# Attention and MLP on one core: two early transfers placed later, and split transfers halved by partitions

## The chip, the core and the metric

The kernel runs on one core of a Trainium2 chip. TensorE (PE) multiplies matrices, ScalarE (ACT) and VectorE (DVE) work on tiles in the on-chip memory of 128 partitions, and SyncE (SP) issues the transfers, which 16 DMA engines carry out. The metric is the device time of one execution in microseconds (us); the median of three is compared.

## The reference

Attention with a sigmoid in place of the softmax, on 8 batches and 12 heads of 448 x 64, then an MLP with a sigmoid-weighted middle. The weights and tensors arrive as follows: q, k and v as float32, the two weight matrices as float64.

```python
scores = scale * np.matmul(q, k.transpose(0, 1, 3, 2)) - np.log(S)
attn = 1.0 / (1.0 + np.exp(-scores))
attn_out = np.matmul(attn, v)                      # (8, 12, 448, 64)
x = attn_out.transpose(0, 2, 1, 3).reshape(3584, 768)
h = x @ w_in                                       # 768 x 2048
g = h * (1.0 / (1.0 + np.exp(-1.702 * h)))
out = g @ w_out                                    # 2048 x 768
```

## The kernel before, in words

Heads are taken in pairs: `pairs` counts (b, p), batch and pair within the batch, six pairs to a batch. Two pairs are a unit. A pair's query and key rows arrive as one tile `qkraw` of 128 partitions and 896 columns (`load_pair`), which ACT or DVE rounds and DVE completes with the rest (`split_pair`, tile `qk`). The pair numbers in names: `qkraw_5` is the sixth pair of batch 0, the `qkraw_0` behind it the first of batch 1, so the seventh pair. The values of a unit's four heads are one tile `vraw`, so `vraw_4` is the third unit's.

PE computes scores (`sc`) in groups of six matmul instructions into four PSUM banks in turn; ACT turns each bank into a tile of sigmoids (`a`, `aside`) at line 709; PE multiplies these by the values (`av`, lines 800 and 780). A unit's scores stand in a long run of seven groups, 42 instructions, and the value matmuls behind it. A group can begin when the bank that it writes has been read by its sigmoid, so the fifth group needs the first sigmoid of the run, the sixth the second, the seventh the third, and the first value matmuls (line 800) the fourth.

Beside attention the weights are decoded from float64 (`decode`): a tile `w_8`, `w_9`, ... of 128 partitions and 1536 eight-byte words is loaded, DVE takes its exponent (line 601) and mantissa (lines 619, 622), ACT its sign (line 605), and DVE joins them. The MLP's products are computed afterwards by a scheme with fewer multiplications, out of sums of weight tiles and of activations; it takes most of the time (line 1225) and isn't touched here.

What stands where on ACT, DVE, PE and SP is set by a planner (`Plan.run`): it keeps a clock of its own for each engine and appends each task to its engine's order when it would begin. The chip then runs each engine's instructions strictly in that order. A task may be held back: when `behind` names another task that isn't in the order yet, `emit` puts it into that task's list `held`, and it is written right behind it. The planner's own clock and choices don't change by that. SP's queue is one line of transfers for loads and stores. Each takes one of eight completion semaphores in turn and waits, before it is issued, for the transfer eight places ahead of it; it also waits for the readers of the buffer that it fills.

A few early transfers are issued as two (`parts` of `dma`, line 501): the tile of the third pair (`HALVES`), the first unit's values and the first decoded weight tile, `w_8`.

Of the kernel before, what the change touches and what calls it, by code (L numbers as in the profile page):

```python
# [19 lines left out]
P = 128  # L20
# [4 lines left out]
WARM = 25  # L25
HALVES = ((0, 2),)
VECTOR_ONLY = (16,)

BUFS = dict(
    qk=3, vraw=3, a=6, ax=6, al=1, raw64=2, e=4, qkraw=5, x32=2,  # L30
# [62 lines left out]
class Plan:  # L93
# [4 lines left out]
    def buffer(self, tag):  # L98
        b, ring = Buffer(), self.rings.setdefault(tag, [])
        b.turn = len(ring) % BUFS[tag]  # L100
        b.bank = tag in BANKS
        ring.append(b)
        return b
# [7 lines left out]
    def task(self, engine, cost, emit, deps=(), uses=()):  # L111
        return self.either({engine: cost}, {engine: emit}, deps, uses)
# [214 lines left out]

    def emit(self, t, e):
        if t.behind is not None and not t.behind.begun:
            t.behind.held.append(t.emits[e])  # L330
            return
        t.emits[e]()
        for f in t.held:
            f()

    def keys(self, last):
        out = {id(t): len(t.then) for t in self.tasks}
# [57 lines left out]
def sigmoid_attention_mlp(ctx: ExitStack, tc: tile.TileContext, qk, v, w, out):  # L395
    nc = tc.nc
# [86 lines left out]
    def held(b, name, n=None, at=0):  # L483

        def view():
            i, start = b.slot
            if i not in arenas:
                arenas[i] = (late_pool(i - 1) if i else sb).tile([P, AREAS[i] * GRAIN], F32, tag=f"arena{i}", name=f"arena{i}", bufs=1)
            start = start * GRAIN + at
            return arenas[i][:, start : start + (n or SIZES[b.kind] * GRAIN)]  # L490

        return view

    def dma(into, src, kb, deps, uses, first=lambda: None, parts=1):
        def emit():
            first()
            to, at = into(), src()
            n = to.shape[-1] // parts
            for i in range(parts):
                cols = slice(i * n, to.shape[-1] if i == parts - 1 else (i + 1) * n)  # L500
                nc.sync.dma_start(out=to[..., cols] if parts > 1 else to, in_=at[..., cols] if parts > 1 else at)

        return task("SP", kb, emit, deps, uses)

    def on_either(act, dve, deps, uses, first=lambda: None):


        def emit(f):
            def go():
                first()  # L510
                f()

            return go

        return either({"ACT": act[0], "DVE": dve[0]}, {"ACT": emit(act[1]), "DVE": emit(dve[1])}, deps, uses)
# [55 lines left out]
    kept = [{v: dram.tile([P, 2, NW_EL], F32, name=f"k{m}_{v}", tag=f"k{m}_{v}") for r, u in enumerate(W_USES)  # L571
             if not X_OF[0][r] for v in parts_of(u)} for m in range(2)]
    whole = [dram.tile([P, 2 * NW_EL], F32, name=f"f{i}", tag=f"f{i}") for i in range(NW)]
    stored, decoded = {}, {}
    N2 = 2 * NW_EL

    def decode(n):

        raw, e, sg = buffer("raw64"), buffer("e"), buffer("e")
        f = plan.slot()  # L580
        f.vital = n < NW // 2
        f32 = held(f, f"w32_{n}", N2)

        def take():
            make(raw, "raw64", [P, 2 * N2], F32, f"w64_{n}")

        def words():
            r = raw.tile.bitcast(U64)
            pair = r.bitcast(U32).rearrange("p (n t) -> p n t", t=2)
            top = r.bitcast(U16).rearrange("p (n t) -> p n t", t=4)[:, :, 3]  # L590
            return pair[:, :, 0], pair[:, :, 1], top

        pair = int(PACE * len(decoded))
        load = dma(lambda: raw.tile.bitcast(U64), lambda: w[n], 4 * KB, [firsts[pair - LEAD]] if pair >= LEAD else [],
                   [raw], take, 1 + (not decoded))
        load.landing += 1.5
        plan.early.append((load, firsts[min(4 + pair, len(firsts) - 1)]))

        def exponent():
            make(e, "e", [P, N2], U16, f"expo{n}")  # L600
            nc.vector.tensor_scalar(e.tile, words()[2], 0x7FF0, None, op0=ALU.bitwise_and)

        def sign():
            make(sg, "e", [P, N2], BF16, f"sign{n}")
            nc.scalar.activation(sg.tile, words()[2].bitcast(I16), AF.Sign)

        t_e = task("DVE", 0.96, exponent, [load], [e, raw])
        t_s = task("ACT", 1.56, sign, [load], [sg, raw])
        t_b = task("DVE", 0.56, lambda: nc.vector.tensor_scalar(
            e.tile, e.tile, 896.0 * 16, 1151.0 * 16, op0=ALU.max, op1=ALU.min), [t_e], [e])  # L610
        t_x = on_either(
            (1.48, lambda: nc.scalar.activation(e.tile, e.tile, AF.Copy, scale=8.0, bias=-896.0 * 128)),
            (0.56, lambda: nc.vector.tensor_scalar(
                e.tile, e.tile, 896.0 * 16, 8.0, op0=ALU.subtract, op1=ALU.mult)),
            [t_b], [e],
        )
        t_g = task("DVE", 0.96, lambda: nc.vector.tensor_tensor(
            e.tile.bitcast(BF16), e.tile.bitcast(BF16), sg.tile, op=ALU.mult), [t_x, t_s], [e, sg])
        t_m = task("DVE", 0.96, lambda: nc.vector.tensor_scalar(
            f32().bitcast(U32), words()[1], 0xFFFFF, 0x100000, op0=ALU.bitwise_and, op1=ALU.bitwise_or  # L620
        ), [load], [f, raw])
        t_l = task("DVE", 1.76, lambda: nc.vector.scalar_tensor_tensor(
            f32(), words()[0], 2.0**-32, f32().bitcast(I32), op0=ALU.mult, op1=ALU.add), [t_m], [f, raw])
        t_p = task("DVE", 1.76, lambda: nc.vector.scalar_tensor_tensor(
            f32(), f32(), 2.0**-20, e.tile.bitcast(BF16), op0=ALU.mult, op1=ALU.mult), [t_l, t_g], [f, e])
        t_m.anytime = True
        if RANKED:
            plan.early += [(t, firsts[min(RANKED + pair, len(firsts) - 1)]) for t in (t_e, t_s, t_b, t_x, t_g, t_m, t_l, t_p)]
        decoded[n] = [Node(f, held(f, f"w32_{n}", N2), [t_p])] if n < NW // 2 else [
            Node(f, held(f, f"w32_{n}", NW_EL, k * NW_EL), [t_p]) for k in range(2)]  # L630
        if n >= NW - NW // 4 or n in whole_pieces:
            stored[n] = dma(lambda: whole[n], f32, 2 * KB, [t_p], [f])
# [5 lines left out]
    def load_pair(b, p):  # L638

        tag = "qkraw"  # L640
        qkr = buffer(tag)

        def first():
            if qkr.tile is None:
                make(qkr, tag, [P, S2], F32, f"qkraw{b}_{p}")


        t_q = []
        for cols in (slice(0, S + P), slice(S + P, S2)) if (b, p) == (0, 0) else (slice(0, S2),):
            t_q.append(dma(lambda cols=cols: qkr.tile[:, cols], lambda cols=cols: qk[b, p * P : (p + 1) * P, cols],  # L650
                           P * (cols.stop - cols.start) * 4 / 1024, [], [qkr], first, 1 + ((b, p) in HALVES)))

        if p % 2 == 0:
            vr = buffer("vraw")
            t_v = dma(lambda: vr.tile, lambda: v[b, p // 2], P * VC * 4 / 1024, [], [vr],
                      lambda: make(vr, "vraw", [P, VC], F32, f"vraw{b}_{p}"), 1 + (b == p == 0))
            v_of[b, p // 2] = t_v, vr
        t_v, vr = v_of[b, p // 2]
        return t_q, qkr, t_v, vr

# [2 lines left out]
    def split_pair(b, p, t_q, qkr):  # L663
        if (b, p) == (0, 0):
            return t_q[0], qkr
        s = buffer("qk")
        parts = [((0.68, 0.455, 0.755), slice(0, S + P)), ((0.41, 0.29, 0.42), slice(S + P, SK))]
        if (b, p) != (0, 1):
            parts = [((0.89, 0.59, 1.02), slice(0, SK))]

        def first():
            if s.tile is None:
                make(s, "qk", [P, 2, SK], F32R, f"qk{b}_{p}")

        for costs, cols in parts:
            t = round_and_rest(
                costs, s, lambda cols=cols: qkr.tile[:, cols], t_q, [qkr],
                lambda cols=cols: s.tile[:, 0, cols], lambda cols=cols: s.tile[:, 1, cols], first,
            )
            begun.append(t)  # L680
            if (b, p) == (0, 4):
                for d in t.deps:
                    d.behind = copies[0]
        return t, s
# [132 lines left out]
    def to_x(b, p, t, ps):  # L817
# [3 lines left out]
        def rows():  # L821
# [3 lines left out]
                      (1.09, lambda: nc.vector.tensor_copy(xb.tile, ps.tile[:, :, :S])), [t], [xb, ps], rows)  # L825
        if len(copies) in VECTOR_ONLY:
            del c.costs["ACT"], c.emits["ACT"]
# [659 lines left out]
    for n in (*range(NW // 2, NW), *needed()):  # L1487
        decode(n)
# [6 lines left out]
    main = []  # L1495
    for one, N, *tables in GROUPS:
        main += group(one, N, *tables, before)
    plan.run((main, side))


# [34 lines left out]
```

## Time and profile before

| | us |
|---|---|
| median of three runs | 1002.72 (1002.42 to 1002.97) |
| profiled execution, its time | 1001.97 |
| its span in the profile | 1000.2 |
| PE busy | 995.9 |
| DVE busy | 874.8 |
| ACT busy | 650.2 |
| DMA queue of SP | 66.1% of 16 engines' span |

The span is what the profile records between the first and the last instruction; the time holds what lies around it too. Matmuls are pipelined, so a PE that is shown as busy may still have stood behind a late weight load for part of a microsecond; that is read from the weight loads (PEld), in whose rows a bracket names the idle time before them and what ended it.

### The profile page before, as it was taken

Reading aid. Unit: us, or ns where it says so; the run is one execution under the profiler, and the core shown is the slowest. Engines: PE = TensorE matmul, PEld = TensorE weight load, DVE = VectorE, ACT = ScalarE, POOL = GpSimd, SP = SyncE. Lnnn points to the kernel's source line nnn. Section 1 sums busy time; section 2 is a strip of 40 time slices with the busy share of each in tenths; the row PEclk is TensorE's granted clock in tenths of the full one; section 3 lists DMA queues with packets and bytes.
Section 4 is the critical chain, followed back from the end, with each engine's and each line's share of the span. In section 5 each row is a group of like instructions: output and inputs, shape, how many; then the busy total and the mean of one; then the engine's idle time right before and its main releaser. Section 6 shows DMA issues by size and latency. Waiting matters only on the chain.

```text
span 1000.2 us, 13998 instructions
## 1 busy us (share of the span) xinstructions
PE 995.9 (100%) x5719; PEld 759.0 (76%) x5719; DVE 874.8 (87%) x596; ACT 650.2 (65%) x527; POOL 0.2 (0%) x4
## 2 busy tenths in 40 slices
PE   9999999999999999999999999999999999999998
PEld 5565555556888888888888888888888888888886
DVE  5999998994999999999997887867898999798885
ACT  7988998885676677666334455765676564455445
POOL 0000000000000000000000000000000000000000
PEclk9999999999999999999999999999999999999999
DMA  9999999997346454445554996545554534566457
GB/s 354 419 399 408 413 406 387 407 385 305 142 177 240 170 214 146 174 155 208 194 196 152 326 299 236 163 156 161 166 176 158 181 100 130 158 190 188 133 184 283
DMA packets 80702, 236.05 MB, mean 236 GB/s; under 512 B 7936, under 2 KB 17792, under 8 KB 78720
## 3 DMA queue, kind: packets, MB, share of 16 engines
q1 hardware_dynamic: 80640, 235.17, 66.1%
q8 instruction: 45, 0.74, 0.3%
q14 instruction: 17, 0.14, 0.0%
HBM read 151.78 MB, written 83.36 MB: 235 GB/s over the span
## 4 chain that ended last, share of the span: by engine, by line
PE 100%; ACT 0%; issue 0%
PE p L1225 74%; PE av L780 10%; PE sc L735 9%; PE av L800 2%; PE sc L751 2%; PE p L983 1%; PE av L764 0%; PE sc L722 0%; PE still L448 0%; ACT arena L1362 0%
## 5 line engine op out<-in xcount | busy, mean ns | idle before, releaser
L1225 PE MATMUL p<-xp,wsplit 128*128 128x512 f32 x1656 | 376.8, 389 | 0.0
L1225 PE MATMUL p<-gp,wsplit 128*128 128x512 f32 x1620 | 368.2, 389 | 0.0
L1225 PEld LDWEIGHTS p<-xp,wsplit 128*128 128x128 f32 x1656 | 310.5, 188 | 65.7 <-issue 0.7
L1225 PEld LDWEIGHTS p<-gp,wsplit 128*128 128x128 f32 x1620 | 304.0, 188 | 63.2 <-DVE gp L1195 0.2
L1392 ACT COPY arena<-p 128x2048 f32<-128x2048 f32 (+1 forms) x70 | 117.3, 1677 | 163.6 <-PE p L1225 146.5
L1183 ACT CAST gp<-arena 128x2048 fp32r<-128x2048 f32 x45 | 86.0, 1912 | 64.0 <-PE p L1225 61.8
L917 DVE TENSOR_TENSOR arena<-arena 128x1536 f32<-128x1536 f32 (+2 forms) x76 | 124.6, 1654 | 2.0 <-DMA arena<-xd 1.2
L1426 DVE TENSOR_TENSOR arena<-arena,p 128x2048 f32<-128x2048 f32 (+1 forms) x44 | 89.4, 2042 | 36.5 <-ACT arena L1392 21.5
L1195 DVE TENSOR_TENSOR gp<-arena,gp 128x2048 fp32r<-128x2048 f32 x45 | 103.0, 2289 | 12.4 <-ACT gp L1183 11.9
L917 DVE TENSOR_TENSOR arena<-arena,arena 128x2048 f32<-128x2048 f32 (+2 forms) x52 | 96.7, 1876 | 4.3 <-DMA xd<-x 3.8
L735 PEld LDWEIGHTS sc<-qk 64*128 64x128 f32 x846 | 77.3, 184 | 21.9 <-issue 9.9
L735 PE MATMUL sc<-qk 64*128 64x448 f32 x846 | 92.2, 368 | 0.0
L1195 DVE TENSOR_TENSOR xp<-arena,xp 128x1536 fp32r<-128x1536 f32 x43 | 75.4, 1753 | 17.8 <-ACT xp L1183 17.7
L709 ACT ACTIVATE aside<-sc 128x896 f32<-128x896 f32 x90 | 78.3, 940 | 15.5 <-PE sc L751 14.4
L1183 ACT CAST xp<-arena 128x1536 fp32r<-128x1536 f32 x42 | 62.2, 1482 | 27.0 <-PE p L1225 20.4
L709 ACT ACTIVATE a<-sc 128x896 f32<-128x896 f32 x78 | 66.1, 944 | 8.7 <-PE sc L735 5.6
L939 DVE TENSOR_TENSOR wsplit<-arena,wsplit 128x1536 fp32r<-128x1536 f32 (+1 forms) x44 | 61.1, 1389 | 5.6 <-ACT wsplit L936 5.6
L936 ACT CAST wsplit<-arena 128x1536 fp32r<-128x1536 f32 (+1 forms) x42 | 49.2, 1172 | 16.3 <-PE p L1225 14.9
L780 PE MATMUL av<-a,vraw 64*64 64x448 f32 x576 | 58.4, 536 | 0.0
L1434 ACT ACTIVATE arena<-arena 128x2048 f32<-128x2048 f32 x26 | 49.7, 1920 | 7.1 <-DVE arena L1426 7.1
L780 PE MATMUL av<-aside,vraw 64*64 64x448 f32 x528 | 53.6, 536 | 0.0
L1426 DVE TENSOR_TENSOR arena<-arena,arena 128x1536 f32<-128x1536 f32 (+1 forms) x25 | 48.9, 1965 | 2.2 <-ACT arena L1392 2.1
(55 smaller groups left out, 610.2 us busy)
## 6 DMA issues: line engine op xcount, KB each, us to landing
wsplit<-c SPq DMA_DIRECT2D x70, 768.0 KB, 4.7
c<-wsplit SPq DMA_DIRECT2D x42, 768.0 KB, 5.0
w<-w SPq DMA_DIRECT2D x15, 1536.0 KB, 11.1
qkraw<-qk SPq DMA_DIRECT2D x46, 448.0 KB, 9.4
wsplit<-f SPq DMA_DIRECT2D x38, 384.0 KB, 3.1
f<-arena SPq DMA_DIRECT2D x14, 768.0 KB, 9.0
c<-arena SPq DMA_DIRECT2D x14, 768.0 KB, 10.4
arena<-xd SPq DMA_DIRECT2D x14, 768.0 KB, 7.0
```

What stands on the lines that cost most here:

```text
L709: nc.scalar.activation(a.tile, ps.tile[:, :, :S], AF.Sigmoid, bias=neg_log_s, scale=scale)
L735: nc.tensor.matmul(ps.tile[:, j, :S], lhsT=src[kk][rows, S + c * P : S + (c + 1) * P], rhs=src[qq][rows, :S], start=i == 0, stop=i == len( ...
L780: now = nc.tensor.matmul(ps.tile[cols, m, :S], lhsT=vr.tile[rows, at : at + D], rhs=two[m][1].tile[rows, j], start=False, stop=turn == 1 a ...
L917: return task("DVE", cost, lambda: nc.vector.tensor_tensor(out(), x(), y(), op=op), deps, uses)
L936: t_hi = on_either((act(n), lambda: nc.scalar.copy(into(0), src())), (cast(n), lambda: nc.vector.tensor_copy(into(0), src())), [*node.done ...
L939: t_lo = task("DVE", dve(n), lambda: nc.vector.tensor_tensor(into(1), src(), into(0).bitcast(F32), op=ALU.subtract), [t_hi], [*bs, node.b])
L1183: t_hi = on_either((act(n), lambda: nc.scalar.copy(part(0)(), node.view())), (cast(n), lambda: nc.vector.tensor_copy(part(0)(), node.view())),
L1195: nc.vector.tensor_tensor(part(1)(), node.view(), part(0)().bitcast(F32), op=ALU.subtract)
L1225: nc.tensor.matmul(ps.tile[:, i], lhsT=into()[:, a, c * P : (c + 1) * P], rhs=xb.tile[:, d, k], start=starts and s == j == 0, stop=ends an ...
L1392: t = on_either((act(self.n), lambda: nc.scalar.copy(view(), node.view())), (dve(self.n), lambda: nc.vector.tensor_copy(view(), node.view())),
L1426: nc.vector.tensor_tensor(view(), x.view(), y.view(), op=ALU.add if s0 == s else ALU.subtract)
L1434: t = task("ACT", act(GB), lambda: nc.scalar.activation(view(), node.view(), AF.Gelu_apprx_sigmoid, scale=float(sign)), [*node.done, *(nod ...
```

## The change

It has two parts. First, a list `LATER` names three tasks that are put behind another one: the load of `w_9` behind that of the seventh pair's `qkraw_0`; the load of `vraw_4` behind that of `w_9`; and DVE's exponent of `w_9` behind the rest of the seventh pair's `qk_0`. `emit` holds a task back together with its engine, so that held tasks can hold others. Second, `dma` with two parts cuts the tile by partitions (64 and 64, whole rows) where it cut by columns before (128 partitions, half rows).

```diff
+LATER = (("w", 9), ("q", 1, 0)), (("v", 0, 2), ("w", 9)), (("e", 9), ("t", 1, 0))
...
     def emit(self, t, e):
         if t.behind is not None and not t.behind.begun:
-            t.behind.held.append(t.emits[e])
+            t.behind.held.append((t, e))
             return
         t.emits[e]()
-        for f in t.held:
-            f()
+        for x in t.held:
+            self.emit(*x)
...
             first()
-            to, at = into(), src()
-            n = to.shape[-1] // parts
-            for i in range(parts):
-                cols = slice(i * n, to.shape[-1] if i == parts - 1 else (i + 1) * n)
-                nc.sync.dma_start(out=to[..., cols] if parts > 1 else to, in_=at[..., cols] if parts > 1 else at)
+            to, at, n = into(), src(), P // parts
+            for rows in [slice(i * n, (i + 1) * n) for i in range(parts)] if parts > 1 else []:
+                nc.sync.dma_start(out=to[rows], in_=at[rows])
+            if parts == 1:
+                nc.sync.dma_start(out=to, in_=at)
...
+        marked["w", n] = load
...
+        marked["e", n] = t_e
...
+        marked["q", b, p] = t_q[-1]
...
+            marked["v", b, p // 2] = t_v
...
+            marked["t", b, p] = t
...
+    for t, other in LATER:
+        marked[t].behind = marked[other]
     plan.run((main, side))
```

On SP's queue, near its start, the rows of before are these, from the first unit's values to the ninth pair's tile; a row is a transfer into a tile, with its partitions and columns, and x2 stands for two of them.

```order
L501 DMA vraw_0_192<-v 128x448 x2
L501 DMA qkraw_2_195<-qk 128x448 x2
L501 DMA qkraw_3_198<-qk 128x896
L501 DMA w_8_200<-w 128x768 x2
L501 DMA qkraw_4_208<-qk 128x896
L501 DMA vraw_2_210<-v 128x896
L501 DMA vraw_4_219<-v 128x896
L501 DMA w_9_240<-w 128x1536
L501 DMA qkraw_5_286<-qk 128x896
L501 DMA qkraw_0_297<-qk 128x896
L501 DMA qkraw_1_309<-qk 128x896
L501 DMA qkraw_2_315<-qk 128x896
```

The same place in the changed kernel:

```order
L500 DMA vraw_0_192<-v 64x896 x2
L500 DMA qkraw_2_195<-qk 64x896 x2
L502 DMA qkraw_3_198<-qk 128x896
L500 DMA w_8_200<-w 64x1536 x2
L502 DMA qkraw_4_208<-qk 128x896
L502 DMA vraw_2_210<-v 128x896
L502 DMA qkraw_5_282<-qk 128x896
L502 DMA qkraw_0_293<-qk 128x896
L502 DMA w_9_295<-w 128x1536
L502 DMA vraw_4_297<-v 128x896
L502 DMA qkraw_1_309<-qk 128x896
L502 DMA qkraw_2_315<-qk 128x896
```

`vraw_4` and `w_9` moved two places down, past `qkraw_5` and `qkraw_0`, and changed places with each other; three tiles are in halves of 64 partitions. All rows behind these are the same in both.

On DVE, where `w_9` is first read (`expo`), before:

```order
L613 TENSOR_SCALAR expo_319<-expo_319 128x1536
L617 TENSOR_TENSOR expo_319<-expo_319,sign_317 128x1536
L601 TENSOR_SCALAR expo_414<-w_9_240 128x1536
L533 TENSOR_TENSOR qk_5_412<-qkraw_5_286,qk_5_412 128x832
L533 TENSOR_TENSOR qk_0_421<-qkraw_0_297,qk_0_421 128x832
L624 SCALAR_TENSOR_TENSOR arena_364<-arena_364,expo_319 128x1536
```

And in the changed kernel:

```order
L616 TENSOR_SCALAR expo_319<-expo_319 128x1536
L620 TENSOR_TENSOR expo_319<-expo_319,sign_317 128x1536
L534 TENSOR_TENSOR qk_5_412<-qkraw_5_282,qk_5_412 128x832
L534 TENSOR_TENSOR qk_0_419<-qkraw_0_293,qk_0_419 128x832
L603 TENSOR_SCALAR expo_433<-w_9_295 128x1536
L627 SCALAR_TENSOR_TENSOR arena_364<-arena_364,expo_319 128x1536
```

The exponent of `w_9` moved behind the rests of the sixth and the seventh pair. ACT's and PE's orders are the same in both: on ACT the casts of `qk_5` and `qk_0`, one sigmoid, the sign of `w_9`, a copy and the sigmoids of the next run follow one another.

## Rows read from the trace of the kernel before

**Rows 1.** The page, part 1: busy us, share of the span, instructions.

```profile
PE 995.9 (100%) x5719; PEld 759.0 (76%) x5719; DVE 874.8 (87%) x596; ACT 650.2 (65%) x527; POOL 0.2 (0%) x4
```

**Rows 2.** The page, part 4: the chain that ended last.

```profile
PE 100%; ACT 0%; issue 0%
```

**Rows 3.** Timeline of PE, 15 to 32 us: start, length, what, how many.

```profile
15.73 4.52 PE L735 MATMUL sc<-qk 64*128 64x448 f32 x42
20.18 0.98 PE L800 MATMUL av<-aside,vraw 64*64 64x448 f32 x8
...
23.24 0.93 PE L751 MATMUL sc<-qkraw 64*64 64x448 f32 x8
...
26.35 5.13 PE L735 MATMUL sc<-qk 64*128 64x448 f32 x42
```

**Rows 4.** Timeline of PE's weight loads, 28.9 to 31.6 us; idle before in brackets.

```profile
29.00 0.51 PEld L735 LDWEIGHTS sc<-qk 64*128 64x128 f32 x6 [0.32 <-ACT a L709]
...
31.43 0.21 PEld L800 LDWEIGHTS av<-aside,vraw 64*64 64x64 f32 x8 [0.32 <-ACT a L709]
```

**Rows 5.** Timeline of ACT, 14 to 32 us.

```profile
14.89 1.63 ACT L605 ACTIVATE sign<-w 128x1536 bf16<-128x1536 int16 x1 [0.27 <-DMA w<-w]
16.64 4.97 ACT L709 ACTIVATE aside<-sc 128x896 f32<-128x896 f32 x6
21.44 0.98 ACT L709 ACTIVATE a<-sc 128x896 f32<-128x896 f32 x1
23.00 0.89 ACT L527 CAST qk<-qkraw 128x832 fp32r<-128x832 f32 x1 [0.58 <-DMA qkraw<-qk]
24.13 0.89 ACT L527 CAST qk<-qkraw 128x832 fp32r<-128x832 f32 x1 [0.24 <-DMA qkraw<-qk]
24.92 0.91 ACT L709 ACTIVATE aside<-sc 128x896 f32<-128x896 f32 x1
25.73 1.61 ACT L605 ACTIVATE sign<-w 128x1536 bf16<-128x1536 int16 x1
27.24 0.89 ACT L824 COPY x<-av 128x896 f32<-128x896 f32 x1
28.03 4.15 ACT L709 ACTIVATE a<-sc 128x896 f32<-128x896 f32 x5
```

**Rows 6.** Timeline of DVE, 0 to 60 us.

```profile
14.90 0.96 DVE L601 TENSOR_SCALAR expo<-w 128x1536 uint16<-128x1536 uint16 x1 [2.54 <-DMA w<-w]
```

**Rows 7.** Timeline of SP's queue, 4 to 10 us: when transfers are issued.

```profile
4.02 0.43 SPq L501 DMA_DIRECT2D qkraw<-qk  x1
...
4.97 0.66 SPq L501 DMA_DIRECT2D w<-w  x1
...
8.25 0.33 SPq L501 DMA_DIRECT2D w<-w  x1
...
9.13 0.33 SPq L501 DMA_DIRECT2D qkraw<-qk  x1
```

**Rows 8.** DMA issues at 4.02, 4.97, 8.25, 9.13: KB, us to landing.

```profile
qkraw<-qk SPq DMA_DIRECT2D x1, 448.0 KB, 6.1
...
w<-w SPq DMA_DIRECT2D x1, 768.0 KB, 9.8
...
w<-w SPq DMA_DIRECT2D x1, 1536.0 KB, 13.6
...
qkraw<-qk SPq DMA_DIRECT2D x1, 448.0 KB, 13.8
```

**Rows 9.** Windows: engines' busy us; last three: granted clock, DMA share, GB/s.

```profile
2.00:3.00 1.00, 1.00 (x12) 1.00 (x11) 0.00 (x0) 0.21 (x2) 0.00 (x0) 1.00 0.85 290
3.00:8.00 5.00, 4.98 (x43) 2.12 (x43) 1.56 (x3) 2.69 (x4) 0.00 (x0) 1.00 0.95 305
8.00:14.80 6.80, 6.80 (x72) 3.44 (x73) 3.15 (x4) 4.30 (x6) 0.00 (x0) 1.00 1.01 410
16.00:22.00 6.00, 6.00 (x62) 4.41 (x64) 5.96 (x7) 5.88 (x8) 0.00 (x0) 1.00 1.02 420
```

**Rows 10.** The first pair's score matmuls, line 722: ns min/median/max.

```profile
L722 PE MATMUL sc<-qkraw x24: 536/536/1003, 3.6 to 6.2; 64*64 64x448 f32 x24
```

More of the change, by code (lines that the diff above doesn't have):

```diff
@@ L573, in sigmoid_attention_mlp @@
     whole = [dram.tile([P, 2 * NW_EL], F32, name=f"f{i}", tag=f"f{i}") for i in range(NW)]
-    stored, decoded = {}, {}
+    stored, decoded, marked = {}, {}, {}
     N2 = 2 * NW_EL
```

## The prediction

> **What bounds the kernel now.** I read the page first, for one question: does any engine limit the whole span? TensorE (PE) is busy for all but 4 us [rows 1], and the chain that ended last runs through PE and nothing else [rows 2]. So the end moves only by microseconds in which PE is made to wait, or no longer waits. PE's own work isn't touched by this change: the same matmuls stand in the same order.
>
> Then I read PE's timeline of the first 50 us, where the changed transfers lie, to find waits that the busy share hides. A run of 42 score matmul instructions takes 4.45 us from its start to the value matmuls that follow (15.73 to 20.18), but the second such run takes 5.08 (26.35 to 31.43) [rows 3, 4]. The extra 0.6 us is a wait for ScalarE (ACT): the weight loads inside and behind that run start about 0.3 us late each, put down to a sigmoid [rows 4]. The reader should see why in ACT's own timeline: its instructions run strictly in their order, and it stood still for 0.58 and 0.24 us until a query/key tile had landed, for the two casts of the sixth and seventh pair at 23.00 and 24.13 [rows 5]. Everything behind them on ACT, the five sigmoids from 28.03 on too, came that much later.
>
> The same view shows a second place where ACT is nearly late: it waited 0.27 us until the first weight tile (w_8) had landed, and started its sign at 14.89 [rows 5]. VectorE waited 2.54 us for the same tile [rows 6]. Behind that sign stand the sigmoids of the run at 15.73. How much later may w_8 come at no cost? The sign ended at 16.52 and the first sigmoid began at 16.64: 0.12 us. Six sigmoids take 4.97, so they start 0.81 apart, and the fourth ends at 16.64 + 3 x 0.81 + 0.92 = 19.99. In the second run the value matmuls started 0.05 behind the end of the fourth sigmoid (28.03 + 2.43 + 0.92 = 31.38, weight load at 31.43 [rows 4, 5]); here they started 0.19 behind it, so 0.14 is spare. Together 0.26 us; beyond that each microsecond that w_8 is late is one of PE's.
>
> Last I read the transfers: issue times [rows 7], time to landing [rows 8] and the rate [rows 9]. The queue is never empty here; the 16 DMA engines are at a share of about 1. The fourth pair's query/key tile (qkraw_3) lands at 4.02 + 6.1 = 10.12, the second half of w_8 at 4.97 + 9.8 = 14.77, the second weight tile w_9 at 8.25 + 13.6 = 21.85, and the sixth pair's qkraw_5 at 9.13 + 13.8 = 22.93. They land in the order of issue, each with the whole backlog before it.
>
> **The change, part by part.** *Part one, the later places.* w_9 (1536 KB) and the third unit's values (448 KB) go behind qkraw_5 and the seventh pair's qkraw_0. Nothing is added. The two query/key tiles then have 1984 KB less before them; at 410 GB/s [rows 9] that is 4.9 us, so they would land near 18 and 19 instead of 22.93 and about 24. ACT wants the first at 21.44 + 0.98 = 22.42, so both its waits go, 0.82 us. What is won is bounded by the stall: 0.6 us, if the sigmoids start at least 0.6 sooner. Between the casts and the sigmoids stand one sigmoid (24.92), the sign of w_9 (25.73) and a copy (27.24). The sigmoid waits for PE's scores at 23.24, which take 0.93, so it can begin near 24.3, 0.6 sooner. I take 0.6, with 0 as the other end. w_9 itself takes over the place where qkraw_5 ended, about 22.9; its sign would start near 25.1, so there are 2 us of cover, and if these go, each further microsecond is PE's. VectorE's exponent of w_9, formerly at the head of the two rests of qkraw_5 and qkraw_0, goes behind them; it is the same 0.97 us of work, on an engine with the rests now ready. Nothing. The values are first used behind the run at 26.35, at 31.43; they would land near 24. Nothing.
>
> *Part two, the shape of the halves.* The first values, the third pair's tile (qkraw_2) and w_8 are each two transfers, before and after. Before, each half had 128 partitions and half a row (1792, 1792 and 6144 bytes); after, it has 64 partitions and whole rows (3584, 3584 and 12288 bytes). The number of issues stays, and so do the waits of each. What changes is the rate at which a half moves, and the trace of before has no transfer of 64 partitions. The ends:
>
> Fast end: only the length of a row counts. In the stretch with most of the 1792-byte pieces the rate was 305 GB/s at a DMA share of 0.95, in the stretch of w_8's 6144-byte pieces 410 at 1.01 and in a later one, with whole rows, 420 [rows 9]. Values and qkraw_2 (0.917 MB) would then take 0.917/0.410 = 2.24 us instead of 3.01, and w_8, at the full rate already, nothing less. 0.8 us sooner; but PE didn't wait there, so nothing comes of it.
>
> Slow end: the rate goes with the number of partitions that are written at a time, so half of 410, 205 GB/s. The 2.49 MB in halves then take 12.15 us. How much later is w_8? By the spacing of landings: values and qkraw_2 take 4.48 instead of 3.01 us, w_8 takes 7.67 instead of the 4.65 between qkraw_3 and it, together 4.5. By rates alone (w_8 3.84 before): 5.3. By bytes: to 14.77 the queue had moved 0.29 + 1.53 + 2.78 = 4.6 MB [rows 9], but up to w_8 only 3.87 are wanted, so some engines were ahead by 0.7 MB; if slow halves let the last engine catch up, w_8 lands at 2.0 + 12.15 + 1.38/0.410 = 17.5, 2.7 later. I take 3.6, midway between 2.7 and 4.5, and keep 2.7 and 5.3 as ends.
>
> Which end? For w_8, which is 63% of these bytes, longer rows can't pay, because 6144-byte pieces already ran at the full rate; its only real change is its width, and there the rows are silent: each of them has all 128 partitions. A step in length lies within what they show, a step to half the width lies outside. So I choose the slow end, not with certainty.
>
> [...]
>
> *The sum.* w_8 late by 3.6, less 0.26 of slack, less 0.6 won at the second run: +2.7 us. Where does the stall go next? ACT and VectorE shift with PE by almost the same amount, and so does the queue, so later stages stand to each other as before; with PE busy to the end nothing gives it back. The profiled execution took 1001.97 us, its span 1000.2; it becomes 1004.7. The median of the three runs is 0.75 above the profiled one, so I predict 1002.72 + 2.7 = **1005.4 us**.
>
> **The rivals.** *Rows count, not partitions* (the fast end). For it: 305 against 410 GB/s shows that the length matters. Against: w_8 is already fast. Only the 0.6 remains: 1002.1 us. This one ends on the other side, not slower; it decides as soon as a half moves faster than about 218 GB/s (2.49 MB then take 11.4 us, w_8 is 2.86 late and PE loses 2.0; that is 0.2%, about what a measurement of this kernel can tell from no change).
>
> *The halves overlap*: engines that are ahead start on the second half while others write the first. For it: the 0.7 MB of lead. Between 218 and 410 GB/s, 1002.1 to 1004.7.
>
> *The second weight tile comes too late instead*: w_9's sign at 25.1 would become the wait. Against it: 2 us of cover. Landing 3 us late it would cost 1 us: 1003.1 beside the first rival.
>
> *The clock falls in the stall.* PE would stand still for almost 3 us before the fifth of the seven groups of the run at 15.73 (ready at 18.28, first sigmoid done at 21.04). [...] At the start of the kernel the longest score matmul took 1003 ns against 536 later [rows 10], so work at half speed is visible there. If it falls, some 2 us of matmuls are done at the lower level: another 1 to 2 us, 1007.
>
> *Faster than 0.2%* needs over 2 us of waits to remove; the first 50 us hold 0.6.
>
> **How the numbers follow.** Slow halves 0.52, of which 0.1 with the clock; full rate 0.33; overlap 0.10, mostly within 0.2%; a late w_9 0.02; something faster 0.03. Slower by over 0.2%: 0.53, within: 0.44, faster: 0.03. The likeliest case's own range is 1004.5 (2.7 late) to 1007.7 (5.3 late without the gain, which is 1007.76, or 3.6 with the clock). Both signs of "slower or not" hold much, so the range reaches from the first rival's 1001.9 to 1007.7.
>
> **What would show it.** In the changed kernel's trace: the landing time of w_8's second half (18.4 forecast; near 14 for the first rival) and the sign behind it; the GB/s between 8 and 15 us (near 205 or near 410); the value matmuls behind the first long run (20.18 before, 23.5 forecast); the next long run back at 4.45 instead of 5.08; casts at 23.00 and 24.13 without a DMA wait. I am wrong if w_8 lands by 15, or if its lateness meets work that ACT could do first.

## The result and the profile after

| | before | changed |
|---|---|---|
| median, us | 1002.31 (1001.79 to 1002.97, 6 runs) | 1010.3 (1007.38 to 1011.24, 6 runs) |
| profiled execution, its time | 1001.97 | 1010.69 |
| its span | 1000.2 | 1008.9 |

The changed kernel is slower, by a ratio of 1.0074 [1.0063, 1.0085]. That is above the range of the prediction: the direction came out as forecast, the size is almost three times the 2.7 us.

Part 1 of the page of the changed kernel, beside [rows 1], and part 4, beside [rows 2]:

```profile
PE 999.3 (99%) x5719; PEld 762.0 (76%) x5719; DVE 874.9 (87%) x596; ACT 650.3 (64%) x527; POOL 0.2 (0%) x4
...
PE 97%; DMA 2%; SPq 0%; DVE 0%; issue 0%; ACT 0%; DVEq 0%
```

TensorE's busy time grew by 3.4 us with the same 5719 instructions, so part of the loss is slower matmuls. The chain that ended last now starts with a transfer. Followed over its first 45 us (start, length, what) it says which one and what stood behind it:

```profile
5.78 16.52 DMA w<-w
...
22.40 0.96 DVE expo L603
23.36 1.01 DVE x L831
24.41 4.85 PE sc L741 x20
```

The second half of `w_8` landed at 22.3 instead of 14.77 [rows 8]. VectorE's exponent waited for it, and behind that the copy of the first unit's value sums (`x`, line 831), and behind that TensorE. The timeline of TensorE, beside [rows 3]:

```profile
17.42 2.09 PE L741 MATMUL sc<-qk 64*128 64x448 f32 x18
24.41 4.85 PE L741 MATMUL sc<-qk 64*128 64x448 f32 x24 [4.91 <-DVE x L831]
29.19 1.23 PE L806 MATMUL av<-aside,vraw 64*64 64x448 f32 x8
...
35.61 4.58 PE L741 MATMUL sc<-qk 64*128 64x448 f32 x42
40.12 0.98 PE L806 MATMUL av<-aside,vraw 64*64 64x448 f32 x8
```

The first long run is torn after three groups of six. The bracket names the copy: the fourth group writes the bank that held those sums. So a group waits for the last reader of its bank, and that isn't always a sigmoid. The timeline of ScalarE, beside [rows 5]:

```profile
22.39 1.62 ACT L607 ACTIVATE sign<-w 128x1536 bf16<-128x1536 int16 x1 [6.13 <-DMA w<-w]
23.88 4.14 ACT L715 ACTIVATE aside<-sc 128x896 f32<-128x896 f32 x5
...
30.12 1.66 ACT L528 CAST qk<-qkraw 128x832 fp32r<-128x832 f32 x2
...
34.40 1.64 ACT L607 ACTIVATE sign<-w 128x1536 bf16<-128x1536 int16 x1
```

The sign of `w_8` began 7.5 us later than before; the two casts and the sign of `w_9` wait for no transfer now. The windows, with granted clock, DMA share and GB/s at the end of a row, beside [rows 9]:

```profile
2.00:3.00 1.00, 1.00 (x12) 1.00 (x11) 0.00 (x0) 0.22 (x2) 0.00 (x0) 1.00 0.75 269
3.00:8.00 5.00, 4.92 (x36) 1.88 (x36) 0.41 (x1) 1.32 (x3) 0.00 (x0) 1.00 0.98 259
8.00:14.80 6.80, 6.39 (x62) 3.63 (x62) 3.33 (x6) 4.86 (x6) 0.00 (x0) 1.00 1.07 224
14.80:20.00 5.20, 4.71 (x48) 3.07 (x40) 1.06 (x2) 0.92 (x1) 0.00 (x0) 1.00 0.98 203
...
24.00:26.00 2.00, 1.59 (x8) 1.45 (x10) 1.97 (x4) 2.00 (x4) 0.00 (x0) 0.50 1.05 432
26.00:28.00 2.00, 2.00 (x14) 1.73 (x14) 2.00 (x3) 2.00 (x3) 0.00 (x0) 0.50 0.99 419
```

From 8 to 20 us, while the halves of the third pair's tile and of `w_8` move, the rate is 203 to 224 GB/s, where it was 410; the DMA share near 1 doesn't show it. When TensorE goes on, its clock is granted at 0.50 (1.00 in [rows 9]).

**The books.** The value matmuls behind the first long run started 9.01 us late (29.19 against 20.18). The second long run took 4.51 instead of 5.08 (0.57 back), and between the two 0.25 more went, mostly while the clock was still low. That is 8.69 at 40.12 (31.43 before), and the spans differ by 8.7. Nothing behind 40 us took part.

### The profile page after: what moved, and what is told of

Same layout as the page of the kernel before. It is cut to its first block, busy times and chain, and to the rows that moved or that the text cites. A ratio compares the mean times of both kernels' runs of the same rounds, so it can differ in the third digit from the quotient of the medians.

```text
span 1008.9 us, 13998 instructions
## 1 busy us (share of the span) xinstructions
PE 999.3 (99%) x5719; PEld 762.0 (76%) x5719; DVE 874.9 (87%) x596; ACT 650.3 (64%) x527; POOL 0.2 (0%) x4
## 4 chain that ended last, share of the span: by engine, by line
PE 97%; DMA 2%; SPq 0%; DVE 0%; issue 0%; ACT 0%; DVEq 0%
PE p L1231 74%; PE av L786 10%; PE sc L741 9%; PE av L806 2%; PE sc L757 2%; DMA w<-w 2%; PE p L989 1%; PE av L770 0%; SPq L500 0%; SPq L502 0%; DVE x L831 0%; DVE expo L603 0%; ACT arena L1368 0%; DVEq L603 0%
## 5 line engine op out<-in xcount | busy, mean ns | idle before, releaser
L1189 ACT CAST xp<-arena 128x1536 fp32r<-128x1536 f32 x42 | 62.2, 1482 | 27.5 <-PE p L1231 20.5
```

The source lines that it names most:

```text
L1189: t_hi = on_either((act(n), lambda: nc.scalar.copy(part(0)(), node.view())), (cast(n), lambda: nc.vector.tensor_copy(part(0)(), node.view())),
```

## The experiments

All twelve are in one table, in us. "Sign" is the start of ScalarE's sign of `w_8`, "first values" and "second values" the value matmuls behind the first and the second long run, each against before (14.89, 20.18, 31.43), "span" against 1000.2; these come from one execution of each. The ratio is that of the times, to before on the same chip.

| run | sign | first values | second values | span | ratio |
|---|---|---|---|---|---|
| change | +7.50 | +9.01 | +8.69 | +8.7 | 1.0074 [1.0063, 1.0085] |
| e11 change again | +7.00 | +8.35 | +7.80 | +7.7 | 1.0076 [1.0062, 1.0090] |
| e2 partition halves only | +6.75 | +8.26 | +8.09 | +8.1 | 1.0075 [1.0061, 1.0089] |
| e3 only w_8 in such halves | +4.00 | +4.93 | +4.37 | +4.4 | 1.0038 [1.0023, 1.0054] |
| e6 w_8 in quarters | +4.09 | +3.68 | +3.15 | +3.8 | 1.0039 [1.0024, 1.0054] |
| e5 only v in such halves | +1.83 | +1.47 | +0.92 | +0.9 | 1.0001 [0.9991, 1.0011] |
| e4 every second partition | +0.35 | +0.72 | +0.16 | +0.1 | 0.9996 [0.9987, 1.0005] |
| e10 the same, old places | +0.26 | +0.64 | +0.07 | +0.1 | 1.0000 [0.9990, 1.0009] |
| e1 later places only | +0.59 | +0.64 | +0.07 | +0.1 | 0.9996 [0.9987, 1.0005] |
| e8 nothing split | +0.26 | +0.02 | -0.54 | -0.3 | 1.0002 [0.9993, 1.0011] |
| e7 readers moved behind | +8.59 | +4.80 | +5.83 | +6.6 | 1.0053 [1.0038, 1.0068] |
| e9 filler | +5.72 | +5.34 | +4.79 | +7.9 | 1.0073 [1.0053, 1.0093] |
| e12 filler again | +7.02 | +6.63 | +6.08 | +7.3 | 1.0070 [1.0057, 1.0082] |

### Which part of the change costs: e1 and e2

Each has one part of the change. e1 is the changed kernel with the column halves of before; e2 is the kernel before with the new `dma`, and no `LATER`. The diff is e1's, against the changed kernel.

```diff
-            to, at, n = into(), src(), P // parts
-            for rows in [slice(i * n, (i + 1) * n) for i in range(parts)] if parts > 1 else []:
-                nc.sync.dma_start(out=to[rows], in_=at[rows])
-            if parts == 1:
-                nc.sync.dma_start(out=to, in_=at)
+            to, at = into(), src()
+            n = to.shape[-1] // parts
+            for i in range(parts):
+                cols = slice(i * n, to.shape[-1] if i == parts - 1 else (i + 1) * n)
+                nc.sync.dma_start(out=to[..., cols] if parts > 1 else to, in_=at[..., cols] if parts > 1 else at)
```

> The later places alone, halves by columns as before. Theory: they win the 0.6 us of the second long run (26.35 to 31.43 becomes 4.5 us long) and cost nothing, 1001.7 against 1002.3, and no transfer rate changes (410 GB/s from 8 to 14.8 us). Rival: the later places share in the loss, because the second weight tile's sign or the third unit's values come too late; then it is over 1003 and a wait of ACT or PE for one of them shows behind 25 us.

> The halves by partitions alone, transfers in their old places. Theory: nearly the whole loss comes from here: 8 to 9.5 us slower than before, near 1011, with the first weight tile landing near 22.3 instead of 14.8, the rate near 205 GB/s from 8 to 20 us and the granted clock at 0.50 for some us behind the stall. Rival: both parts of the change are needed for the loss; then this one is under 4 us slower.

e2 costs all of it: +8.1 of span, with 204 GB/s from 12 to 18 us. e1 is no different from before in time. Its TensorE, and then its ScalarE:

```profile
26.99 4.57 PE L741 MATMUL sc<-qk 64*128 64x448 f32 x42
31.50 0.98 PE L806 MATMUL av<-aside,vraw 64*64 64x448 f32 x8
```

```profile
22.87 1.72 ACT L528 CAST qk<-qkraw 128x832 fp32r<-128x832 f32 x2
```

The second long run takes 4.51 (5.08 before [rows 3]) and the casts no longer wait [rows 5]. That looks like the gain as forecast, but it isn't yet one: in this execution the second pair's tile landed 0.6 us later than in that of before, so the first long run began at 16.37. e10 (below) has the old places and the same late start, and there the second run takes 4.51 too; in e2, also with the old places, it takes 4.54. When TensorE and ScalarE come to the casts later, less of the waits is left: in e10 none at the first cast and 0.23 us at the second (0.58 and 0.24 in [rows 5]). So where TensorE comes that late anyway, the later places win nothing; what they win where it is on time, e8 shows.

### Place or width: e4, e10 and e6

e4 is the changed kernel with halves of 64 partitions that lie apart, every second one; e10 has the same halves and the old places. e6 loads only `w_8` in pieces by partitions, four of 32 neighbours, and the rest by columns.

```diff
-            for rows in [slice(i * n, (i + 1) * n) for i in range(parts)] if parts > 1 else []:
+            for rows in [slice(i, None, parts) for i in range(parts)] if parts > 1 else []:
```

> As the change, but each half takes every second partition (0, 2, 4, ... and 1, 3, 5, ...), so it has 64 partitions and whole rows too, spread over the whole memory. Theory of place (a half of neighbouring partitions is slow because all engines write into one half of the memory): fast, 400 GB/s from 8 to 14.8, the weight tile by 15, 1001.7 to 1002.5. Rival of width (any 64 partitions move at half the rate): as the change, near 205 GB/s and 1010.

> Halves of every second partition, in the old places of the queue. With the later places the time was 1002.03. Theory (the later places win 0.6 us at most, halves of this shape nothing): 1002.0 to 1002.7, with the two casts on ScalarE waiting for query and key tiles as before. Rival: the whole rows win time, under 1001.7.

> Later places kept; the first weight tile in four transfers of 32 neighbouring partitions, values and third pair's tile in column halves. Theory of place: 32 neighbouring partitions move as fast as 64, so the rate from 8 to 14.8 us and the landing near 18.9 are those of the run with halves, and the time is 1005.5 to 1007. Rival (the rate goes with the number of partitions): near 100 GB/s, landing past 24, over 1010.

The window from 11 to 14 us lies inside the load of `w_8` (in e4 from 10.7 to 14.4), in e6 but for its first 0.5 us. First e4, then e6, then e3 (below), whose `w_8` is in halves of 64 neighbours:

```profile
11.00:14.00 3.00, 3.00 (x36) 1.22 (x32) 1.36 (x2) 0.99 (x2) 0.00 (x0) 1.00 0.97 401
```

```profile
11.00:14.00 3.00, 3.00 (x36) 1.22 (x32) 1.62 (x2) 1.10 (x2) 0.00 (x0) 1.00 0.99 213
```

```profile
11.00:14.00 3.00, 3.00 (x37) 1.22 (x33) 1.51 (x2) 0.69 (x2) 0.00 (x0) 1.00 0.96 209
```

The same 64 partitions in number, and the same 12288 bytes in a row, move at 401 GB/s when they are spread over all 128 and at 209 when they are neighbours; 32 neighbours are no slower than 64 (213). So the rate goes with where the partitions lie, not with how many they are.

One rival has no run of its own: a half of neighbours also reads one closed stretch of the chip's main memory, 768 KB, and e4 reads every second row, so both ends of the transfer differ. Against the reading end speaks that a full-width tile of 448 KB is a closed stretch too, and a shorter one, and that two of them in a row (`qkraw_4`, `vraw_2`) landed at 15.8 and 16.9 in before, 1.1 us apart, which is over 400 GB/s.

### Who else pays: e5 and e3

In both the later places are kept. In e5 only the values are halved by partitions, in e3 only `w_8`; the others go by columns. The diff is e3's; the new last argument of `dma` asks for halves by partitions.

```diff
-                   [raw], take, 1 + (not decoded))
+                   [raw], take, 1 + (not decoded), True)
```

> Later places kept; only the first unit's values in halves of 64 partitions. It tells whether a transfer of full width that is issued before a slow half is slowed by it: in the changed kernel the second pair's tile, issued at 1.65, landed at 7.6 instead of 6.1. Theory (it is slowed): the second pair's tile lands 0.5 us or more later than the 6.0 to 6.7 seen with column halves, the first long run starts near 17, and the time is 1002.5 to 1003.5. Rival (transfers land strictly one behind the other): it lands by 6.7, and the time is 1002.

> Later places kept; only the first weight tile in halves of 64 partitions, the first values and the third pair's tile in halves by columns. Theory (each half of 64 neighbouring partitions moves at some 205 GB/s, and the full-width transfers beside it are slowed too): the weight tile lands 3.5 to 4.5 us late (18.3 to 19.3), the second pair's tile on time at 6.1, PE loses 3 to 4 us less the 0.6, and a stall that short may leave the clock up: 1004.5 to 1006. Rival (the weight tile alone carries the loss): over 1008.

In e5, the transfer issued just ahead of the values, the second pair's tile with all 128 partitions, took this long from its issue at 1.64 (KB, us):

```profile
qkraw<-qk SPq DMA_DIRECT2D x1, 448.0 KB, 5.9
```

In before it took 4.4. That is more than scatter: in the seven traces with the values in halves of neighbours, this one among them, it took 5.4 to 6.3, on average 5.8; in the seven without 4.3 to 5.2, on average 4.8. In e3 the third pair's halves go by columns, and the tile behind them, `qkraw_3`, again 128 partitions wide, landed 6.9 us after its issue instead of 6.1 [rows 8], with the slow `w_8` behind it; in e6 it took 7.5, in e1, with `w_8` by columns, 6.2. The time of e3, 1006.27, is just above its expectation: its clock fell all the same (last section). Transfers of full width lose time beside the halves, those ahead of them too.

### The clock and the copy: e9, e11, e12 and e7

e9 is the changed kernel with 72 small matmuls behind the third group, into columns of its bank that nobody reads; the output stays the same. e12 is e9 again, on one chip with e11, the change again.

```diff
+            for i in range(FILL if (n, c) == (2, 2) else 0):
+                nc.tensor.matmul(
+                    ps.tile[:, 0, S:], lhsT=still, rhs=still[:, : 512 - S], start=True, stop=True, skip_group_check=True)
```

> As the change, with 72 small matmuls between the third and the fourth group of the first long run, which write an unused strip of a bank and are no part of the result; they keep TensorE working through the time in which it would wait. Theory (2.4 us of the loss are the clock): the granted clock stays at 1.00 from 20 to 30 us, the fourth group starts at the same time as in the changed kernel, the four groups behind it take 2.6 to 3.5 us instead of 4.8, and the time is 1007.5 to 1008.5. Rival (those groups are slow because they wait for sigmoids): no gain, 1010.

> The changed kernel once more, with a second trace, beside the next run on the same chip. Both theories: 1007 to 1011; the loss all lies ahead of 45 us, and PE doesn't wait for VectorE between 200 and 420 us.

> The run with 72 small matmuls in the stall once more, beside the change on the same chip. Theory (given back later: a queue and a VectorE that are late by 6 to 8 us bind PE again at 50 and at 270 us as soon as PE itself is less late): the four slow groups are fast again, but PE waits 1 to 3 us more behind 50 us, and the time is within 1 us of the change's. Rival (the first run of this was an accident of one execution): the time is 1.5 to 2.5 us under the change's.

e11 and e12 have the sign at the same moment, 21.89 and 21.91, and the fourth group at 23.92 and 23.93. TensorE's timeline of e11:

```profile
23.92 4.68 PE L741 MATMUL sc<-qk 64*128 64x448 f32 x24 [4.87 <-DVE x L831]
28.53 0.98 PE L806 MATMUL av<-aside,vraw 64*64 64x448 f32 x8
```

and of e12:

```profile
23.93 2.95 PE L742 MATMUL sc<-qk 64*128 64x448 f32 x24 [1.59 <-DVE x L835]
26.81 0.98 PE L810 MATMUL av<-aside,vraw 64*64 64x448 f32 x8
```

With the filler the granted clock stays at 1.00 from 20 to 30 us, and the same four groups take 2.88 from their start to the value matmuls instead of 4.61. So the clock's price is 1.7 us here, and 1.9 in the change (4.78). But the time doesn't show it: medians of 1009.74 and 1009.15, ranges that overlap, spans 0.4 apart. Of e9 the table shows where it went: +4.79 at the second values, +7.9 at the end. Put beside before, matmul by matmul, TensorE loses 0.9 of these 3.1 in the run at 53.02, where a group waits for a sigmoid (5.39 us to the value matmuls instead of 4.45), 1.7 near 270 us, and 0.5 more are lost behind its last product. e12 loses 0.8 near 270 us and 0.4 at the end. Waits of e9 between 250 and 290 us (who for whom: us in total, times, longest):

```profile
ACT xp L1193 <- DMA arena<-xd: 2.5, 1, 2.5
...
DVE xp L1205 <- ACT xp L1193: 1.8, 1, 1.8
PE p L1235 <- DVE xp L1205: 1.2, 1, 1.2
```

A transfer, ScalarE, VectorE, TensorE: a chain that is late for its own reasons. e12 has the same wait, of 0.6. Neither the changed kernel nor e11 has such a wait of TensorE behind 40 us; with TensorE held up longer in front, the others have caught up by then.

e7 is the changed kernel with the readers of `w_8` moved: VectorE's exponent behind the rest of the fifth pair, and so behind the copy, and ScalarE's sign behind the sixth sigmoid of the run (that of `w_9` behind the sigmoids of the second long run too).

```diff
-LATER = (("w", 9), ("q", 1, 0)), (("v", 0, 2), ("w", 9)), (("e", 9), ("t", 1, 0))
+LATER = (("s", 9), ("a", 6, 1)), (("e", 8), ("t", 0, 4)), (("s", 8), ("a", 3, 2)), (("w", 9), ("q", 1, 0)), (("v", 0, 2), ("w", 9)), (("e", 9), ("t", 1, 0))
```

> As the change, but what reads the late weight tiles first stands further back: VectorE's exponent of w_8 behind the copy of the value sums and the fifth pair's rest, ScalarE's sign of w_8 behind the six sigmoids of the first long run, its sign of w_9 behind those of the second. Theory: the wait moves but does not go, since the whole queue is late: the fifth pair's tile lands near 23.2, its rest is ready near 25, and the last of the seven groups of the first long run waits for it, 3 to 4 us instead of the 4.9 and the slow groups behind it. 1006 to 1008.5. Rival (only the instructions queued behind the two reads of w_8 cost time): the first long run isn't interrupted, 1003.5 to 1004.5.

TensorE's timeline, and under it VectorE's:

```profile
17.76 3.98 PE L742 MATMUL sc<-qk 64*128 64x448 f32 x36
24.18 0.87 PE L742 MATMUL sc<-qk 64*128 64x448 f32 x6 [2.44 <-DVE qk L534]
24.98 1.77 PE L808 MATMUL av<-aside,vraw 64*64 64x448 f32 x8
```

```profile
22.38 0.59 DVE L529 CAST qk<-qkraw 128x832 fp32r<-128x832 f32 x1 [3.40 <-DMA qkraw<-qk]
```

The stop in front of the fourth group is gone, and six groups run through. The next one waits for the fifth pair's tile, the transfer behind `w_8` in the queue, and the clock falls all the same (0.66 from 25 to 30 us). The two readers alone are not the cause; the whole queue is late. 1 to 2 us are won against e11 and the change, +6.6 remains.

### Without any split: e8

The changed kernel with `parts` at 1 for all three tiles.

```diff
-                   [raw], take, 1 + (not decoded))
+                   [raw], take, 1)
...
```

> Later places, and none of the three tiles split: one transfer each with all partitions and whole rows. Theory (place is all that matters, and all partitions are written): the rates of before or better, the first weight tile by 15, 1001.5 to 1002.5. Rival (splitting itself buys an earlier landing of the first tiles): the second or third pair's tile lands over 0.5 later, 1002.5 to 1004.

In its profiled execution the second pair's tile landed as early as in before and the first values are on time (+0.02). Here the later places' gain is seen by itself: 0.54 us at the second values, 0.3 at the end. That execution was the fastest of its eleven; their median, 1002.60, is no different from before. It lies where the rival of the expectation began, but the rival's sign is absent: the second and the third pair's tile landed 0.0 and 0.2 us later than in before.

## Why the prediction was right in direction and wrong in size

**The mechanism held.** "Half of 410, 205 GB/s" was measured as 203 to 224. Full rate and overlap, two of the rivals, are excluded by that and by the landing at 22.3, and the late `w_9` by its sign at 34.40, which waits for nothing.

**The basis was half wrong.** "The rate goes with the number of partitions that are written at a time" gave the right number for the wrong property: e4 has as few partitions in a transfer and is fast, and e6 has fewer still and isn't slower.

**Step that failed first: how late `w_8` is.** 3.6 was forecast, 7.5 measured. Landing after landing, the lateness grows like this: at the second pair's tile 1.50, over the values and `qkraw_2` 1.66 more (1.47 forecast by the spacing), over `qkraw_3` 0.96, over `w_8` 3.41 (3.02 forecast). The halves cost 5.1, close to the 4.5 of the working; the two tiles of full width cost 2.5, and they were not in the sum at all. From these the issues and landings of the changed kernel can be read, the tiles issued at 1.65, 4.00 and 4.64:

```profile
qkraw<-qk SPq DMA_DIRECT2D x1, 448.0 KB, 5.9
...
qkraw<-qk SPq DMA_DIRECT2D x1, 224.0 KB, 8.2
...
qkraw<-qk SPq DMA_DIRECT2D x1, 448.0 KB, 9.6
```

e5 and e3 show the neighbours' loss with one tile in halves at a time. How much of the 1.50 is this and how much the scatter of 0.9 among the traces without such halves can't be told from one execution. But the term is there in each of the other five traces with all three tiles in such halves (e2, e7, e9, e11, e12): `w_8` landed at 20.5 to 21.8 in them, 5.7 to 7.0 late, the halves cost 3.1 to 4.8 of it and the two full-width tiles 1.8 to 3.6. The profiled execution of the change is the latest of the six. Worse than the omission was the lower end: "slow halves let the last engine catch up" counted the 0.7 MB of lead as a gain, and the midpoint of 2.7 and 4.5 was drawn down by it. The lead stayed: from 2.00 to 22.30 the queue moved 4.8 MB (236 GB/s), of which the same 3.87 were wanted, so 0.9.

Of the 6.0 us between the forecast 2.7 and the 8.7 of the span, 3.9 are this step and 1.9 the clock (below).

**Step that held: "beyond that each microsecond that `w_8` is late is one of PE's".** In e6, e9 and e12, where the clock stayed up, the first values are later by the sign's lateness less 0.41, 0.38 and 0.39. The spare time was 0.4 instead of 0.26. In the change it gives 7.50 - 0.4 = 7.1, and the clock's 1.9 makes the 9.0 that were measured. In e11 7.00 - 0.4 + 1.7 = 8.3 (8.35), in e2 6.75 - 0.4 + 1.9 = 8.25 (8.26).

**Step missed: where TensorE stops.** It was to stop before the fifth group, and stopped before the fourth, for VectorE's copy behind the exponent. VectorE's wait had been read [rows 6], but not what stood behind it; the text ahead of the prediction, too, lets a group wait for sigmoids alone. At the full clock the copy costs nothing of its own: 24.41 + 2.88 = 27.29, while ScalarE's fourth sigmoid, by the working's spacing, ends at 23.88 + 2.43 + 0.92 = 27.23. It put one more group into the slow stretch.

**The rival that came true beside the likeliest: the clock.** It was sized rightly (1 to 2 us; 1.7 and 1.9 measured) and held too unlikely. In the changed kernel it came on top of the stop. What the sum doesn't say is that a cure for it alone wins almost nothing, as e12 shows.

**The gain of 0.6** was 0.54 in e8, where everything ahead of it was on time. In the changed kernel the sum's -0.6 came in (0.57), but not from the later places: with TensorE 0.64 late the second run took 4.51 in e1 and in e10, so ScalarE's waits for the casts did not reach it there, wherever the tiles stand in the queue. In no run did the later places alone change the time by more than the measurement can tell, and 0.06% is less than that.

**Still open:** which of the 16 engines keep the full-width tiles back; why e9 waits for a sigmoid at 53 us and e12 doesn't; and whether the lateness of 0.6 to 0.7 us at the second pair's tile in e1, e4 and e10 has another cause than scatter.

## What to carry to other kernels

Cut a transfer so that each piece spans the whole range of partitions, by columns (411 GB/s from 11 to 14 us in before) or by every second partition (401 in e4, 209 with neighbours in e3), and count as slowed every transfer that shares the queue with a piece that doesn't (the second pair's tile took 5.8 us instead of 4.8 on average). For each tile that comes late, list what stands behind its first reader on every engine, the copies that free a bank above all (4.91 us of wait behind one in the changed kernel), and not only the reader named in the wait. When a stop of TensorE is removed or its clock is kept up, look further down for the next chain that is just as late before counting the gain.

## What was not expected of the hardware

The DMA share was 0.96 at 209 GB/s (e3) and 0.97 at 401 (e4): it says that the engines have work, not that they move it fast. The time from issue to landing of the second pair's tile scattered between 4.3 and 5.2 us over the seven traces in which the values are not in halves of neighbours, which is more than the gain under study. And in e3 a pause of 3.23 us was followed by a granted clock of 0.50 from 22 to 24 us, while in e6 one of 2.47 us left it at 1.00. TensorE's timelines of e3 and of e6:

```profile
20.92 4.26 PE L746 MATMUL sc<-qk 64*128 64x448 f32 x24 [3.23 <-DVE x L836]
25.11 0.98 PE L811 MATMUL av<-aside,vraw 64*64 64x448 f32 x8
```

```profile
21.02 2.91 PE L746 MATMUL sc<-qk 64*128 64x448 f32 x24 [2.47 <-DVE x L836]
23.86 0.98 PE L811 MATMUL av<-aside,vraw 64*64 64x448 f32 x8
```

The four groups take 4.19 at the lower level and 2.84 at the upper, though the sign of `w_8` was 4 us late in both. At the end of the span only 0.6 of these 1.35 us are left, and the medians of the two runs, 1006.27 and 1006.76, don't show it; e6's profiled execution was the fastest of its four. Nor does the length of the pause decide by itself: e7's, of 2.44 us, is no longer than e6's, and the granted clock was 0.66 from 25 to 30 us behind it.
